# Induced-set attention with a maxout layer: maxima swapped by GpSimd, a column of ones beside x, and a short softmax kept in PSUM

## The chip, the cores and the metric

The kernel runs on one core of a Trainium2 chip. The metric is the device time of one execution in microseconds, as a median over runs. Below, PE is TensorE's matrix unit, PEld its loading of weights, DVE is VectorE, ACT is ScalarE, POOL is GpSimd and SP is SyncE, which here only issues DMAs.

## The reference

Four batches of 12544 tokens with 128 channels attend to 32 inducing points, which have first attended to the tokens; a maxout layer of width 768 follows. All of it is float32.

```python
B, N, m, C = (4, 12544, 32, 128)

def mab(q, kv):
    s = scale * (q @ kv.transpose(0, 2, 1))
    s = s - s.max(-1, keepdims=True)
    a = np.exp(s)
    a /= a.sum(-1, keepdims=True) + 1e-09
    return a @ kv
h = mab(I, x)        # I: the inducing points, for every batch
y = mab(x, h)        # tokens attend to the 32 states
# maxout, d_model 128, d_ff 768, on the 50176 rows of y
g = np.maximum(np.maximum(y @ w1, y @ w2), y @ w3)
out = g @ w_out
```

## The kernel before

**Tiles.** A batch has 98 tiles of 128 tokens: a short group of 2 tiles and 6 full groups of 16. x comes twice from HBM: as tokens (`xg`, tokens on partitions) and, for batches 1 to 3, already transposed by the host (`xT`, channels on partitions). For batch 0 PE transposes it. The host changes no value.

**First attention, batch 0 (`phase1_first`).** Before the pipeline starts, groups are taken one by one: load, transpose on PE (`transpose_x`, L270), scores, maxima, exponentials, sums. In between, DVE prepares the weights in a fixed order. Loads are queued in the order `LOADS`. Then the second attention's softmax for the short group and the first full one runs in an order written out by hand (`ORDER`); steps "a" are the short group's, "b" the full one's.

**Main pipeline (`main`, `advance`, `stage2`).** The two halves of the layer are folded, so that a chunk of 512 tokens needs no y: `us` holds the states multiplied by w1 - w2 and w3 - w2, and by the product of w2 and w_out. The 600 slots are 6 blocks of 128 of the layer for each of 100 chunks. In each slot PE multiplies `pu` of the next slot (L758) and `pv` of this one (L764); ACT makes `ru` = relu(pu) (L773); DVE makes `h` = max(pv, ru) (L791); ACT rounds h to `hi` (L780); POOL makes the remainder `lo` = h - hi (L788), or DVE does so in the slots of `LOWVEC` (L794). Six slots later PE adds three products of hi and lo into the chunk's sum (L814 to L816), which L813 has started in the chunk's first slot. `pu`, `pv` and the chunk's sum `acc` have two PSUM banks each; `h` has five buffers, hi and lo have ten.

**Windows.** A window is 24 slots: the four chunks of one full group. In each the next group's softmax goes through DVE and ACT one step at a time (`softmax2` at the slots of `STEPS2`, steps in `scores_steps`), and its result is spread over partitions by SP's DMAs (`probs`, L743). The short group has its own form of the last steps, and a copy of its scores in SBUF (`es`).

**Turns.** The first attention of batches 1 to 3 runs inside the windows, one group (the first turn two groups) at a time, 6 turns a batch, 18 in all. `turn` puts its steps at fixed slots from the window's slot 2 on (for batch 1 also from slot 15): scores on PE (`turn_products`, L363), a negated copy with its minimum per partition (`turn_max`, L381), then the minimum over the four blocks of 32 partitions by two exchanges (`turn_swap` with 64 and then 32 partitions, L401 and L402; `turn_least`, L409 and L413), exponentials (`turn_weights`, L422), a transpose of 32 x 32 blocks (`turn_transpose`, L434). A window later the weighted sums follow (`turn_sums`, L448), and the running sums are rescaled (`turn_keep`: `hs` L463 for the states, `ls` L466 for the sums of weights). At a batch's end `turn_totals` (L479, L480) adds up the blocks. The last batch's windows have no turns.

The order on every engine is the program's own (a manual schedule): an instruction that waits holds all that is behind it on its engine.

Of the kernel before, what the change touches and what calls it, by code (L numbers as in the profile page):

```python
# [8 lines left out]
F32 = mybir.dt.float32  # L9
# [4 lines left out]
ALU = mybir.AluOpType  # L14
# [11 lines left out]
def kernel(ctx, tc, x, xt, ind_t, w1, w2, w3, w_out, out):  # L26
# [43 lines left out]
    xp = ctx.enter_context(tc.tile_pool(name="xp", bufs=2))  # L70
# [36 lines left out]

    xg_next = {}
    xts_free = [const.tile([P, GT * P], F32, name=f"xT{i}", tag=f"xT{i}") for i in range(XTB)]
    xgs_free = [const.tile([P, GT, C], F32, name=f"xg{i}", tag=f"xg{i}") for i in range(XB)]  # L110
    w_space = xts_free.pop()
    shelf = const.tile([P, UW + 2 * groups[0]["nt"] * P + 2 * P + 2 * M + OB * 512], F32, name="shelf")
    shelf_at = [0]

    def place(n):
# [123 lines left out]

    def start_batch(b):  # L240
        st = state[b] = {"xT": {}, "xg": {}, "a": {}, "s": {}}
        st["lst"] = bp.tile([P, NG], F32, name="lst", tag="lst")
        if b == 0:
            st["mneg"] = bp.tile([P, NG], F32, name="mneg", tag="mneg", bufs=1)
            st["hg"] = bp.tile([P, NG, C], F32, name="hg", tag="hg", bufs=1)
        else:
            st["mm"] = bp.tile([P, NK], F32, name="mm", tag="mm")
            st["fac"] = bp.tile([P, NK], F32, name="fac", tag="fac")
            st["hs"] = bp.tile([P, C], F32, name="hs", tag="hs")
            st["ls"] = bp.tile([P, 1], F32, name="ls", tag="ls")  # L250
# [14 lines left out]
    def transpose_x(b, gi, k):  # L265
        st = state[b]
        n = min(4, groups[gi]["nt"] - k)
        tps = (bank_u + bank_v)[k // 4]
        for i in range(n):
            nc.tensor.transpose(out=tps[:, i * P : (i + 1) * P], in_=st["xg"][gi][:, k + i, :], identity=ident)  # L270
# [60 lines left out]
    def attend_sums(b, gi, bank=None):  # L331
        nt = groups[gi]["nt"]
        st = state[b]
        xg, aT = st["xg"].pop(gi), st["a"].pop(gi)
        if nt == GT:
            xgs_free.append(xg)
        st["h"] = hps = bank or spare[0]
        for t in range(nt):
            q = t % NQ
            nc.tensor.matmul(  # L340
                out=hps[q * M : (q + 1) * M, :C],
                lhsT=aT[:, t * M : (t + 1) * M],
                rhs=xg[:, t, :],
                start=(t < NQ),
                stop=(t + NQ >= nt),
            )
# [8 lines left out]
    def turn_products(b, k):  # L355

        st = state[b]
        banks = {}
        for gi in turns[k]:
            w = groups[gi]["nt"] * M  # L360
            bank = bank_a[1] if groups[gi]["nt"] == GT else spare[0][:, C : C + w]
            for q in range(NQ):
                nc.tensor.matmul(  # L363
                    out=bank[q * M : (q + 1) * M, :w],
                    lhsT=iT,
                    rhs=st["xT"][gi][:, q * w : (q + 1) * w],
                    start=True,
                    stop=True,
                )
            banks[gi] = bank[:, :w]  # L370
        st[("s", k)] = banks

    def turn_max(b, k):

        st = state[b]
        a = wk.tile([P, WK], F32, name="a", tag="a")
        mq = wk.tile([P, 3], F32, name="mq", tag="mq")
        at = 0
        for i, (gi, bank) in enumerate(st.pop(("s", k)).items()):
            w = bank.shape[1]  # L380
            nc.vector.tensor_scalar(  # L381
                out=a[:, at : at + w],
                in0=bank,
                scalar1=-1.0,
                scalar2=None,
                op0=ALU.mult,
                op1=ALU.min,
                accum_out=mq[:, i : i + 1],
            )
# [4 lines left out]
        st[("mq", k)] = mq[:, :1], mq[:, 2:]  # L394

    def turn_swap(b, k, step):

        st = state[b]
        mq, other = st[("mq", k)]
        for lo in range(0, P, 2 * step):  # L400
            nc.vector.tensor_copy(out=other[lo : lo + step], in_=mq[lo + step : lo + 2 * step])  # L401
            nc.vector.tensor_copy(out=other[lo + step : lo + 2 * step], in_=mq[lo : lo + step])  # L402

    def turn_least(b, k, last):

        st = state[b]
        mq, other = st[("mq", k)]
        if not last:
            nc.vector.tensor_tensor(out=mq, in0=mq, in1=other, op=ALU.min)  # L409
        elif k == 0:  # L410
            nc.vector.tensor_tensor(out=st["mm"][:, :1], in0=mq, in1=other, op=ALU.min)
        else:
            nc.vector.scalar_tensor_tensor(  # L413
                out=st["mm"][:, k : k + 1], in0=mq, scalar=st["mm"][:, k - 1 : k], in1=other, op0=ALU.min, op1=ALU.min
            )

    def turn_weights(b, k):

        st = state[b]
        a = st[("a", k)]  # L420
        least = st["mm"][:, k : k + 1]
        nc.scalar.activation(out=a, in_=a, func=AF.Exp, bias=least, scale=-1.0, accum_out=st["lst"][:, k : k + 1])  # L422
# [14 lines left out]
    def turn_sums(b, k):  # L437
# [7 lines left out]
        st["h"] = spare[0][:, :C]  # L445
        for t, row in enumerate(rows):
            q = t % NQ
            nc.tensor.matmul(  # L448
# [7 lines left out]
    def turn_keep(b, k):  # L456

        st = state[b]
        if k == 0:
            nc.vector.tensor_copy(out=st["hs"], in_=st["h"])  # L460
            return
        fac = st["fac"][:, k : k + 1]
        nc.vector.scalar_tensor_tensor(  # L463
            out=st["hs"], in0=st["hs"], scalar=fac, in1=st["h"], op0=ALU.mult, op1=ALU.add
        )
        nc.vector.scalar_tensor_tensor(  # L466
            out=st["ls"],
            in0=st["ls"] if k > 1 else st["lst"][:, :1],
            scalar=fac,
            in1=st["lst"][:, k : k + 1],  # L470
            op0=ALU.mult,
            op1=ALU.add,
        )
# [206 lines left out]
    def scores_steps(b, gi):  # L680
# [181 lines left out]
    def turn(b, k, s):  # L862

        at(s, turn_products, b, k)
        at(s + 2, turn_max, b, k)
        at(s + 3, turn_swap, b, k, 2 * M)
        at(s + 4, turn_least, b, k, False)
        at(s + 5, turn_swap, b, k, M)
        at(s + 6, turn_least, b, k, True)
        at(s + 7, turn_weights, b, k)  # L870
        at(s + 9, turn_transpose, b, k)

    def window(i):
        return (i // (NG - 1)) * per_batch + short + (i % (NG - 1)) * WIN
# [18 lines left out]
    for n in range(1, B):  # L893
# [144 lines left out]
```

## Time and profile before

| | |
|---|---|
| median of 3 runs | 851.65 us (850.05 to 854.28) |
| profiled execution | 854.22 us, of which span 852.4 us |
| PE, ACT, DVE, POOL busy | 96%, 87%, 79%, 75% |
| granted TensorE clock | 0.991 |
| loads of x (L94) | 23 of 1024 KB, 4 of 256 KB, 4 of 128 KB |

The span runs from the first to the last instruction of one profiled execution. A group line names line, engine, operation, tiles and shapes, then the busy time, the mean of one in ns, and the idle time of the engine just before them with what ended it. A timeline row starts with start and duration in us. Matmuls are pipelined and their ends are modelled, so PE's start times say more than its busy time.

### The profile page before, as it was taken

The page shows a single profiled execution, that of the slowest core. Times are in us where ns is not written, and L with a number is a line of the kernel's source. Part 1 is how long each engine was busy: PE and PEld are TensorE (multiplying, and loading weights), DVE is VectorE, ACT ScalarE, POOL GpSimd, SP SyncE. Part 2 cuts the span into 40 slices and gives each one's busy share as a digit, 9 for nine tenths or more (in the row PEclk, how much of TensorE's full clock was granted, in tenths as well). Part 3 has the DMA queues.
Part 4 walks back from the last instruction along what each step waited for, and adds up shares of the span by engine and source line. Part 5 has one row for each costly group of instructions (what it writes and reads, how often), then busy time and mean ns, then how long its engine had stood idle before and what let it go on. Part 6 is the DMA issues. An engine that isn't in the chain of part 4 may idle for free.

```text
span 852.4 us, 14763 instructions
## 1 busy us (share of the span) xinstructions
PE 821.6 (96%) x4530; PEld 623.8 (73%) x4530; DVE 675.7 (79%) x1238; ACT 744.3 (87%) x1508; POOL 636.2 (75%) x509
## 2 busy tenths in 40 slices
PE   6879999999999999999999999999999999999998
PEld 4646776777777777777677677777778778778786
DVE  5958788787886977878888779788788788777864
ACT  5748898988988989989889789898899899999996
POOL 0027687877877878878768778787789888888886
PEclk9979999999999999999999999999999999999999
DMA  9406643335453343353355343431423222222221
GB/s 345 163 22 201 211 164 109 122 105 170 123 151 120 102 159 121 102 179 119 97 155 161 119 130 100 167 121 48 131 71 93 75 75 67 64 75 75 72 77 50
DMA packets 44061, 102.50 MB, mean 120 GB/s; under 512 B 9552, under 2 KB 13264, under 8 KB 38736
## 3 DMA queue, kind: packets, MB, share of 16 engines
q1 hardware_dynamic: 43984, 101.57, 37.1%
q8 instruction: 36, 0.59, 0.3%
q14 instruction: 41, 0.34, 0.1%
HBM read 48.12 MB, written 25.69 MB: 87 GB/s over the span
## 4 chain that ended last, share of the span: by engine, by line
PE 78%; DVE 15%; issue 3%; ACT 2%; POOL 1%; DMA 1%; SPq 0%; DVEq 0%; ACTq 0%; POOLq 0%
PE pv L764 14%; PE acc L814 14%; PE acc L815 13%; PE acc L816 13%; PE pu L758 13%; DVE h L791 5%; PE aux L675 3%; PE acc L813 2%; PE acc L448 2%; PE aux L363 2%; DVE aux L695 1%; DVE a L381 1%; DVE mx L693 1%; DVE mq L401 1%; DVE mq L402 1%
## 5 line engine op out<-in xcount | busy, mean ns | idle before, releaser
L788 POOL TENSOR_TENSOR lo<-h,hi 128x512 fp32r<-128x512 f32 (+1 forms) x498 | 630.9, 1296 | 157.4 <-ACT hi L780 100.0
L791 DVE TENSOR_TENSOR h<-pv,ru 128x512 f32<-128x512 f32 (+1 forms) x600 | 401.8, 673 | 142.9 <-PE pv L764 93.4
L773 ACT ACTIVATE ru<-pu 128x512 f32<-128x512 f32 (+1 forms) x600 | 372.2, 620 | 59.5 <-PE pu L758 56.0
L780 ACT CAST hi<-h 128x512 fp32r<-128x512 f32 (+1 forms) x600 | 383.2, 639 | 15.6 <-DVE h L791 12.9
L764 PE MATMUL pv<-pT,us 128*128 128x512 f32 (+1 forms) x600 | 238.4, 397 | 12.2 <-DVE h L791 11.4
L758 PE MATMUL pu<-pT,us 128*128 128x512 f32 (+1 forms) x600 | 232.8, 388 | 3.3 <-ACT hi L780 1.9
L814 PE MATMUL acc<-hi,wo_hi 128*128 128x512 f32 (+1 forms) x600 | 235.4, 392 | 0.0
L815 PE MATMUL acc<-hi,wo_lo 128*128 128x512 f32 (+1 forms) x600 | 232.0, 387 | 0.0
L816 PE MATMUL acc<-lo,wo_hi 128*128 128x512 f32 (+1 forms) x600 | 231.7, 386 | 0.0
L764 PEld LDWEIGHTS pv<-pT,us 128*128 128x128 f32 x600 | 112.8, 188 | 54.8 <-DVE h L791 34.5
L814 PEld LDWEIGHTS acc<-hi,wo_hi 128*128 128x128 f32 x600 | 113.0, 188 | 40.6 <-issue 20.5
L758 PEld LDWEIGHTS pu<-pT,us 128*128 128x128 f32 x600 | 112.8, 188 | 30.1 <-ACT ru L773 2.3
L816 PEld LDWEIGHTS acc<-lo,wo_hi 128*128 128x128 f32 x600 | 112.9, 188 | 23.5
L815 PEld LDWEIGHTS acc<-hi,wo_lo 128*128 128x128 f32 x600 | 113.0, 188 | 22.4
L794 DVE TENSOR_TENSOR lo<-h,hi 128x512 fp32r<-128x512 f32 x102 | 73.9, 725 | 1.8 <-ACT hi L780 1.0
L821 ACT COPY shelf<-acc 128x512 f32<-128x512 f32 (+1 forms) x100 | 61.0, 610 | 3.0 <-PE acc L816 3.0
L813 PE MATMUL acc<-pT,us 128*128 128x512 f32 (+1 forms) x100 | 39.0, 390 | 0.0
L234 POOL TENSOR_TENSOR wo_lo<-xT,wo_hi 128x768 fp32r<-128x768 f32 x1 | 1.8, 1806 | 39.0 <-ACT wo_hi L233 39.0
L675 PE MATMUL aux<-xT,hT 128*32 128x512 f32 x192 | 26.4, 623 | 0.0
L448 PEld LDWEIGHTS acc<-xg,aT 128*32 128x32 f32 x576 | 16.8, 110 | 8.5 <-issue 5.5
L813 PEld LDWEIGHTS acc<-pT,us 128*128 128x128 f32 x100 | 18.9, 190 | 3.2
L723 DVE TENSOR_TENSOR pl<-aux,ph 128x512 fp32r<-128x512 f32 x24 | 16.5, 688 | 4.2 <-ACT ph L720 4.2
(136 smaller groups left out, 476.3 us busy)
## 6 DMA issues: line engine op xcount, KB each, us to landing
out_dram<-shelf SPq DMA_DIRECT2D x96, 256.0 KB, 2.0
xg<-in_x_dram SPq DMA_DIRECT2D x23, 1024.0 KB, 5.3
xT<-in_xt_dram SPq DMA_DIRECT2D x18, 1024.0 KB, 5.1
pT<-ph SPq DMA_DIRECT2D x192, 64.0 KB, 2.0
pT<-pl SPq DMA_DIRECT2D x192, 64.0 KB, 2.0
raw<-in_w_dram SPq DMA_DIRECT2D x3, 768.0 KB, 11.7
us<-uh SPq DMA_DIRECT2D x24, 52.0 KB, 2.5
us<-ul SPq DMA_DIRECT2D x24, 52.0 KB, 1.9
```

The costliest lines, as they stand in the source:

```text
L758: nc.tensor.matmul(out=pu[:, :w], lhsT=state[c.b]["us"][:, 2 * j * P : (2 * j + 1) * P], rhs=c.pT[:, :w], start=True, stop=True)
L764: nc.tensor.matmul(out=pv[:, : d.w], lhsT=state[d.b]["us"][:, (2 * j + 1) * P : (2 * j + 2) * P], rhs=d.pT[:, : d.w], start=True, stop=True,)
L773: nc.scalar.activation(out=ru[:, :w], in_=pu[:, :w], func=AF.Relu)
L780: nc.scalar.copy(out=hi[:, : c.w], in_=h[:, : c.w])
L788: nc.gpsimd.tensor_sub(**args)
L791: nc.vector.tensor_max(out=h[:, : d.w], in0=pv[:, : d.w], in1=relus.pop(s)[:, : d.w])
L794: nc.vector.tensor_sub(**low)
L813: nc.tensor.matmul(out=c.acc[:, :w], lhsT=us[:, 2 * DF :], rhs=c.pT[:, :w], start=True, stop=False)
L814: nc.tensor.matmul(out=c.acc[:, :w], lhsT=wo_hi[:, j, :], rhs=c.hh[j][:, :w], start=False, stop=False)
L815: nc.tensor.matmul(out=c.acc[:, :w], lhsT=wo_lo[:, j, :], rhs=c.hh[j][:, :w], start=False, stop=False)
L816: nc.tensor.matmul(out=c.acc[:, :w], lhsT=wo_hi[:, j, :], rhs=c.hl[j][:, :w], start=False, stop=(j == NJ - 1))
L821: nc.scalar.copy(out=o[:, : c.w], in_=c.acc[:, : c.w])
```

## The change

Three things are changed together.

1. **Swaps on GpSimd.** The six copies of a turn's exchange go from DVE to POOL. `mq` has room beside each column for what comes from the other block, so that each minimum is one `tensor_reduce` over adjacent columns; in the last one a third column, copied by POOL too, holds the minimum of the turn before. The separate minimum of a turn with two groups is gone. The steps after the first swap move back: the two minima from slots +4 and +6 to +5 and +8, the second swap from +5 to +6, the weights from +7 to +9, the transpose from +9 to +11.
2. **A column of ones.** The tiles of tokens become 129 columns wide, the last set to 1 once at the start, so the loads fill rows of 512 B that are 516 B apart. The turn's weighted sums take all 129 columns, so the last column of `hs` is the sum of weights; `ls`, its rescaling and the accumulating output of the exponentials are gone. The short group's tokens move from a pool of their own to the shelf.
3. **Short softmax in PSUM.** The scores of the short group are transposed in place and stay in PSUM, and its last steps (for batches 1 to 3) come up to three slots earlier.

```diff
+    for xg in xgs_free + [short_x]:
+        nc.gpsimd.memset(xg[:, :, C:], 1.0)
...
-            nc.sync.dma_start(out=xg[:, k : k + n, :], in_=xv[b, :, g["t0"] + k : g["t0"] + k + n, :])
+            nc.sync.dma_start(out=xg[:, k : k + n, :C], in_=xv[b, :, g["t0"] + k : g["t0"] + k + n, :])
...
-        mq = wk.tile([P, 3], F32, name="mq", tag="mq")
+        n = 2 * len(turns[k])
+        mq = wk.tile([P, n + 3], F32, name="mq", tag="mq")
...
-        if len(turns[k]) > 1:
-            nc.vector.tensor_tensor(out=mq[:, :1], in0=mq[:, :1], in1=mq[:, 1:2], op=ALU.min)
+        if k > 0:
+            nc.gpsimd.tensor_copy(out=mq[:, n + 2 :], in_=st["mm"][:, k - 1 : k])
...
     def turn_swap(b, k, step):
-        mq, other = st[("mq", k)]
-        for lo in range(0, P, 2 * step):
-            nc.vector.tensor_copy(out=other[lo : lo + step], in_=mq[lo + step : lo + 2 * step])
-            nc.vector.tensor_copy(out=other[lo + step : lo + 2 * step], in_=mq[lo : lo + step])
+        n = len(turns[k])
+        own, far = (mq[:, :n], mq[:, n : 2 * n]) if step > M else (mq[:, 2 * n : 2 * n + 1], mq[:, 2 * n + 1 : 2 * n + 2])
+        for lo in range(0, P, step):
+            to = lo ^ step
+            nc.gpsimd.tensor_copy(out=far[to : to + step], in_=own[lo : lo + step])
...
     def turn_least(b, k, last):
-        if not last:
-            nc.vector.tensor_tensor(out=mq, in0=mq, in1=other, op=ALU.min)
...
-            nc.vector.scalar_tensor_tensor(
-                out=st["mm"][:, k : k + 1], in0=mq, scalar=st["mm"][:, k - 1 : k], in1=other, op0=ALU.min, op1=ALU.min
-            )
+        n = 2 * len(turns[k])
+        out, cols = (st["mm"][:, k : k + 1], mq[:, n : n + 2 + (k > 0)]) if last else (mq[:, n : n + 1], mq[:, :n])
+        nc.vector.tensor_reduce(out=out, in_=cols, axis=AX.X, op=ALU.min)
...
-        nc.scalar.activation(out=a, in_=a, func=AF.Exp, bias=least, scale=-1.0, accum_out=st["lst"][:, k : k + 1])
+        nc.scalar.activation(out=a, in_=a, func=AF.Exp, bias=least, scale=-1.0)
...
-        nc.vector.scalar_tensor_tensor(
-            out=st["ls"],
-            in0=st["ls"] if k > 1 else st["lst"][:, :1],
...
-        nc.tensor.matmul(out=st["lp"], lhsT=st["ls"].to_broadcast([P, P]), rhs=sel[:, :M], start=True, stop=True)
+        nc.tensor.matmul(out=st["lp"], lhsT=st["hs"][:, C:].to_broadcast([P, P]), rhs=sel[:, :M], start=True, stop=True)
...
-        if nt < GT:
-            flat = wk.tile([P, w], F32, name="es", tag="es", bufs=1)
...
-        nc.vector.transpose(out=flat, in_=sp[:, :w])
+        nc.vector.transpose(out=flat, in_=flat)
...
-        at(s + 4, turn_least, b, k, False)
-        at(s + 5, turn_swap, b, k, M)
-        at(s + 6, turn_least, b, k, True)
-        at(s + 7, turn_weights, b, k)
-        at(s + 9, turn_transpose, b, k)
+        at(s + 5, turn_least, b, k, False)
+        at(s + 6, turn_swap, b, k, M)
+        at(s + 8, turn_least, b, k, True)
+        at(s + 9, turn_weights, b, k)
+        at(s + 11, turn_transpose, b, k)
...
-        softmax2(n, 0, *(s0 + k for k in (17, 18, 19, 20, 21, 22, 23, 24, 26, 28)))
+        softmax2(n, 0, *(s0 + k for k in (17, 18, 19, 20, 21, 22, 23, 23, 24, 25)))
```

More of the change, by code (lines that the diff above doesn't have):

```diff
@@ L109 @@
     xts_free = [const.tile([P, GT * P], F32, name=f"xT{i}", tag=f"xT{i}") for i in range(XTB)]
-    xgs_free = [const.tile([P, GT, C], F32, name=f"xg{i}", tag=f"xg{i}") for i in range(XB)]
+    xgs_free = [const.tile([P, GT, C + 1], F32, name=f"xg{i}", tag=f"xg{i}") for i in range(XB)]
     w_space = xts_free.pop()
-    shelf = const.tile([P, UW + 2 * groups[0]["nt"] * P + 2 * P + 2 * M + OB * 512], F32, name="shelf")
+    shelf = const.tile([P, UW + 2 * groups[0]["nt"] * P + 2 * P + 2 * M + OB * 512 + groups[0]["nt"] * (C + 1)], F32, name="shelf")
     shelf_at = [0]
@@ L120 @@
     short_t = [place(groups[0]["nt"] * P) for i in range(2)]
+    short_x = place(groups[0]["nt"] * (C + 1)).rearrange("p (t c) -> p t c", c=C + 1)
+    for xg in xgs_free + [short_x]:
+        nc.gpsimd.memset(xg[:, :, C:], 1.0)
     iT = place(M)
@@ L241, in start_batch @@
         st = state[b] = {"xT": {}, "xg": {}, "a": {}, "s": {}}
-        st["lst"] = bp.tile([P, NG], F32, name="lst", tag="lst")
         if b == 0:
+            st["lst"] = bp.tile([P, NG], F32, name="lst", tag="lst", bufs=1)
             st["mneg"] = bp.tile([P, NG], F32, name="mneg", tag="mneg", bufs=1)
@@ L269, in transpose_x @@
         for i in range(n):
-            nc.tensor.transpose(out=tps[:, i * P : (i + 1) * P], in_=st["xg"][gi][:, k + i, :], identity=ident)
+            nc.tensor.transpose(out=tps[:, i * P : (i + 1) * P], in_=st["xg"][gi][:, k + i, :C], identity=ident)
         xv4 = st["xT"][gi].rearrange("p (q t l) -> p t q l", q=NQ, l=M)
@@ L342, in attend_sums @@
                 lhsT=aT[:, t * M : (t + 1) * M],
-                rhs=xg[:, t, :],
+                rhs=xg[:, t, :C],
                 start=(t < NQ),
@@ L360, in turn_products @@
             w = groups[gi]["nt"] * M
-            bank = bank_a[1] if groups[gi]["nt"] == GT else spare[0][:, C : C + w]
+            bank = bank_a[1] if groups[gi]["nt"] == GT else spare[0][:, 2 * C : 2 * C + w]
             for q in range(NQ):
@@ L390, in turn_max @@
             at += w
-        if len(turns[k]) > 1:
-            nc.vector.tensor_tensor(out=mq[:, :1], in0=mq[:, :1], in1=mq[:, 1:2], op=ALU.min)
         st[("a", k)] = a[:, :at]
-        st[("mq", k)] = mq[:, :1], mq[:, 2:]
+        if k > 0:
+            nc.gpsimd.tensor_copy(out=mq[:, n + 2 :], in_=st["mm"][:, k - 1 : k])
+        st[("mq", k)] = mq
     def turn_swap(b, k, step):
-        st = state[b]
-        mq, other = st[("mq", k)]
-        for lo in range(0, P, 2 * step):
-            nc.vector.tensor_copy(out=other[lo : lo + step], in_=mq[lo + step : lo + 2 * step])
-            nc.vector.tensor_copy(out=other[lo + step : lo + 2 * step], in_=mq[lo : lo + step])
+        n = len(turns[k])
+        mq = state[b][("mq", k)]
+        own, far = (mq[:, :n], mq[:, n : 2 * n]) if step > M else (mq[:, 2 * n : 2 * n + 1], mq[:, 2 * n + 1 : 2 * n + 2])
+        for lo in range(0, P, step):
+            to = lo ^ step
+            nc.gpsimd.tensor_copy(out=far[to : to + step], in_=own[lo : lo + step])
     def turn_least(b, k, last):
         st = state[b]
-        mq, other = st[("mq", k)]
-        if not last:
[L409 to L413, printed above, removed]
-                out=st["mm"][:, k : k + 1], in0=mq, scalar=st["mm"][:, k - 1 : k], in1=other, op0=ALU.min, op1=ALU.min
-            )
+        n = 2 * len(turns[k])
+        mq = st[("mq", k)]
+        out, cols = (st["mm"][:, k : k + 1], mq[:, n : n + 2 + (k > 0)]) if last else (mq[:, n : n + 1], mq[:, :n])
+        nc.vector.tensor_reduce(out=out, in_=cols, axis=AX.X, op=ALU.min)
     def turn_weights(b, k):
@@ L444, in turn_sums @@
                 xgs_free.append(xg)
-        st["h"] = spare[0][:, :C]
+        st["h"] = spare[0][:, : C + 1]
         for t, row in enumerate(rows):
@@ L465, in turn_keep @@
         )
-        nc.vector.scalar_tensor_tensor(
-            out=st["ls"],
-            in0=st["ls"] if k > 1 else st["lst"][:, :1],
[L469 to L473, printed above, removed]
     def turn_totals(b, bank):
@@ L478, in turn_totals @@
         st["lp"], st["sum"] = bank[:, :M], bank[:, M : 2 * M]
-        nc.tensor.matmul(out=st["lp"], lhsT=st["ls"].to_broadcast([P, P]), rhs=sel[:, :M], start=True, stop=True)
-        nc.tensor.matmul(out=st["sum"], lhsT=st["hs"], rhs=sel[:, :M], start=True, stop=True)
+        nc.tensor.matmul(out=st["lp"], lhsT=st["hs"][:, C:].to_broadcast([P, P]), rhs=sel[:, :M], start=True, stop=True)
+        nc.tensor.matmul(out=st["sum"], lhsT=st["hs"][:, :C], rhs=sel[:, :M], start=True, stop=True)
     def phase1_first(weights):
```

6 lines of the change are left out of this document (2 added, 4 removed).

## The prediction

> **What bounds the kernel now.** I read the page first: engine shares, the chain, the groups.
>
> ```profile
> span 852.4 us, 14763 instructions
> PE 821.6 (96%) x4530; PEld 623.8 (73%) x4530; DVE 675.7 (79%) x1238; ACT 744.3 (87%) x1508; POOL 636.2 (75%) x509
> PE 78%; DVE 15%; issue 3%; ACT 2%; POOL 1%; DMA 1%; SPq 0%; DVEq 0%; ACTq 0%; POOLq 0%
> ```
>
> PE is the bound, but 15% of the chain is DVE, so PE waits for it somewhere. A busy PE is no proof of a dense one, so next I compared stretches: a full window (24 slots, one group of tokens) of batch 1, with a turn in it, and one of batch 3, which has none. The timeline's pv records mark where each starts and ends, and the two PE bursts are what a turn adds.
>
> ```profile
> 302.38 0.39 PE L764 MATMUL pv<-pT,us 128*128 128x512 f32 x1
> 335.02 0.39 PE L764 MATMUL pv<-pT,us 128*128 128x512 f32 x1
> 728.16 0.39 PE L764 MATMUL pv<-pT,us 128*128 128x512 f32 x1
> 757.52 0.39 PE L764 MATMUL pv<-pT,us 128*128 128x512 f32 x1
> 306.08 1.06 PE L448 MATMUL acc<-xg,aT 128*32 128x128 f32 x32
> 306.95 1.04 PE L363 MATMUL aux<-xT,shelf 128*32 128x512 f32 x8
> 302.40:335.00 32.60, 32.02 (x173) 24.03 (x172) 26.25 (x50) 29.07 (x59) 25.54 (x21) 1.00 0.40 129
> 728.20:757.50 29.30, 29.30 (x133) 23.32 (x132) 23.17 (x38) 27.93 (x56) 24.60 (x20) 1.00 0.25 73
> ```
>
> The window with a turn takes 335.02 - 302.38 = 32.64 us, the one without 757.52 - 728.16 = 29.36. PE's own work for the turn is 1.06 + 1.04 = 2.10, so 32.64 - 29.36 - 2.10 = 1.18 us is standing. The waits of that window (engine, line, releaser, total, times, longest) and DVE's timeline show where.
>
> ```profile
> PEld pv L764 <- DVE h L791: 1.9, 4, 0.9
> 310.36 5.25 POOL L788 TENSOR_TENSOR lo<-h,hi 128x512 fp32r<-128x512 f32 x4 [2.46 <-PE pu L758]
> 310.97 0.70 DVE L466 SCALAR_TENSOR_TENSOR ls<-ls,fac,lst 128x1 f32<-128x1 f32 x1
> 314.25 0.15 DVE L402 COPY mq<-mq 64x1 f32<-64x1 f32 x1
> 314.43 0.69 DVE L791 TENSOR_TENSOR h<-pv,ru 128x512 f32<-128x512 f32 x1
> 315.04 0.58 DVE L409 TENSOR_TENSOR mq<-mq 128x1 f32<-128x1 f32 x1
> 315.55 0.68 DVE L791 TENSOR_TENSOR h<-pv,ru 128x512 f32<-128x512 f32 x1
> ```
>
> PE waits for h, because pv's two banks come free only when h has read them. L409 works on one column, yet takes 0.58 us and ends at 315.62; POOL's fourth lo ends at 310.36 + 5.25 = 315.61. It stood for POOL. Its range over the run says the same, beside the copies (one input) and the reduction (one input, no wait):
>
> ```profile
> L409 DVE TENSOR_TENSOR mq<-mq x18: 234/580/1300, 74.5 to 582.9; 128x1 f32<-128x1 f32 x18
> L402 DVE COPY mq<-mq x54: 143/147/149, 73.7 to 585.2; 32x1 f32<-32x1 f32 x36, 64x1 f32<-64x1 f32 x18
> L308 DVE TENSOR_REDUCE mneg<-acc x7: 154/156/163, 6.9 to 39.9; 128x1 f32<-128x4 f32 x7
> ```
>
> **The change part by part.** *DVE loses.* Six copies a turn, 6 x 0.147 = 0.88 us; L409 (0.58) and the last minimum L413, both for reductions of 0.16; and L466 (0.70), as the ones column carries the sums of weights through hs.
>
> ```profile
> L413 DVE SCALAR_TENSOR_TENSOR mm<-mq,mm 128x1 f32<-128x1 f32 x15 | 5.7, 383 | 0.0
> L422 ACT ACTIVATION_READ_ACCUMULATOR a<-a,mm 128x1 f32 x18 | 3.4, 186 | 0.0
> L448 PE MATMUL acc<-xg,aT 128*32 128x128 f32 x576 | 19.6, 273 | 0.0
> ```
>
> That is 0.88 + 0.58 + 0.38 + 0.70 - 2 x 0.16 = 2.2 us of DVE a turn, 40 us over 18 turns. It counts only where it ends PE's wait: 18 x 1.18 = 21.2 us at most. ACT sheds 0.186 us a turn (3.4 in all), off the path. The merged minimum of the two-group turns goes with it. Row 129 of L448 costs 19.6/128 = 0.15 us in all; hs with 129 columns nothing.
>
> *POOL gains* six copies of one or two columns a turn and, from k = 1, one more of the old minimum. No row shows such a copy. Bounds: a memset of one column (0.10, nothing read), and what is left at zero width of POOL's two-input lo, from its two forms.
>
> ```profile
> 0.27 0.10 POOL L1018 MEMSET const-float32-1.0<- 128x1 f32 x1
> L788 POOL TENSOR_TENSOR lo<-h,hi 128x512 fp32r<-128x512 f32 x474 | 612.4, 1321 | 153.2 <-ACT hi L780 96.5 <-PE pu L758 43.0 <-PE pv L764 9.4
> L788 POOL TENSOR_TENSOR lo<-h,hi 128x256 fp32r<-128x256 f32 x24 | 18.6, 794 | 4.2 <-ACT hi L780 3.5 <-PE pu L758 0.6
> ```
>
> 0.794 - (1.321 - 0.794) = 0.27. A copy reads one input and carries little, so I take 0.15, nearer the memset. Seven add 1.05 us to a window in which POOL is busy 25.5 of 32.6, but behind them queue the lo products. These follow each other every 5.25/4 = 1.31 us at most, against 1.13 us of a slot on PE (below), so POOL falls behind through slots 3 to 14 anyway. A lo has room: it is made one slot after its h and used six slots after, so the copies should cost PE nothing there.
>
> *The new wait* is DVE's: each reduction stands for POOL's swap, and behind it stand h products. The first swap (issued in slot 5, read in slot 7) arrives in time. The second is issued in slot 8 behind lo of slot 7 and read in slot 10. The POOL row above begins with lo of slot 2, so lo of slot 5 ends at 315.61:
>
> ```profile
> 311.27 0.39 PE L764 MATMUL pv<-pT,us 128*128 128x512 f32 x1
> 300.12 0.39 PE L764 MATMUL pv<-pT,us 128*128 128x512 f32 x1
> 301.25 0.39 PE L764 MATMUL pv<-pT,us 128*128 128x512 f32 x1
> 300.64 0.69 DVE L791 TENSOR_TENSOR h<-pv,ru 128x512 f32<-128x512 f32 x1 [0.38 <-PE pv L764]
> ```
>
> That is 4.34 after its pv (311.27). An undisturbed slot takes 301.25 - 300.12 = 1.13, and 1.36 where a chunk's sum begins (once in slots 5 to 7), so lo of slot 7 ends 4.34 + 2 x 0.18 - 0.23 + 3 x 0.15 = 4.9 after its pv, and the swap 0.6 later, 5.5. Slot 10's pv comes at 3.4 on that count, and its h ends 0.52 + 0.69 later, at 4.6. DVE stands 0.9 us, and h of slot 11, due at 3.4 + 1.13 + 0.52 = 5.05, starts at 5.7, 0.65 late. PE forgives h about 1.0 us: two slots (2.26) less 0.52 and 0.69.
>
> But the reciprocal and the product of the softmax follow in slot 11 and now both transposes in slot 13 (the weights' one moved from slot 11), and ACT, busy 29.07 of 32.60, has little left. So I leave 0.35 us of stall a turn: 18 x 0.35 = 6.3. At 0.10 a copy h is 0.3 late and nothing is left (0); at 0.27 it is 1.5 late, over PE's allowance before the softmax's work comes on top, and about all of 1.18 stays (21).
>
> *Short softmax in PSUM.* It matters at the start, on the chain:
>
> ```profile
> 53.68 1.19 DVE L713 TENSOR_TENSOR pn<-es,pn 128x128 fp32r<-128x128 f32 x1 [1.05 <-ACT pn L711]
> L463 DVE SCALAR_TENSOR_TENSOR hs<-hs,fac,acc x15: 303/306/340, 122.7 to 610.3; 128x128 f32<-128x128 f32 x15
> ```
>
> With one input from PSUM I price it like L463, 0.31: -0.9 us (0 if it keeps its 1.19). In later batches it ends a window before it is wanted.
>
> *x loads.* A row of tokens becomes 516 B apart, so a load of 8 KB a partition becomes 16 pieces of 512 B. No row shows 512 B. These stretches hold loads in 8 KB pieces, in 1 KB pieces (w_out), and the run of the first loads (us, engines' busy and counts, clock, DMA share, GB/s):
>
> ```profile
> 14.00:16.20 2.20, 2.20 (x16) 1.96 (x14) 2.17 (x4) 1.45 (x4) 0.00 (x0) 1.00 0.98 408
> 11.70:13.70 2.00, 2.00 (x10) 0.35 (x3) 0.13 (x1) 0.84 (x3) 0.00 (x0) 1.00 1.14 403
> 2.00:9.00 7.00, 3.55 (x21) 2.85 (x22) 2.76 (x8) 1.50 (x5) 0.00 (x0) 1.00 0.95 330
> 9.00:25.00 16.00, 14.39 (x121) 9.53 (x119) 11.85 (x20) 12.05 (x27) 0.00 (x0) 1.00 0.97 389
> 25.00:33.50 8.50, 8.50 (x120) 5.99 (x116) 8.36 (x14) 6.95 (x16) 0.00 (x0) 1.00 0.69 264
> 26.33 0.87 PE L270 MATMUL pu<-shelf,xg 128*128 128x128 f32 x6
> ```
>
> At full share 408/0.98 = 416 GB/s over 16 engines is 315 ns per 8 KB, and 403/1.14 = 353 is 46 ns per 1 KB. A line through both gives 8 ns a piece and 0.0375 ns a byte, so 27 ns for 512 B: 16 x 27 = 435 ns for 315, +1.0 us per 1 MB group. The ends: 20 ns (no price per piece) and 46 (a piece of 512 B no cheaper than one of 1 KB).
>
> Before, 7 x 330 + 16 x 389 = 8.5 MB are in by 25 us: the weights (3.1) and x through group 5 (5.4). Five groups then land 4.7 us later. Group 5's transposes start at 26.33, so 1.3 us of that is slack. From 25 to 33.5 DVE is busy 8.36 of 8.5 with weight preparation in fixed order and absorbs about another 1.1. I take +2.3 us (0 to +15, at 46 ns). Steady loads of x run slots ahead, at a DMA share of 0.40: nothing. The six memsets of ones precede the identity on POOL, about 0.6 us before its first use at 4 us: nothing, +0.5 if loads wait for them.
>
> The Trainium skill (DMA: Bandwidth & Descriptors, Specifications) gives 512 B as the least transfer at line rate; by it the x loads would cost 0 and the sum 2.3 less. No run here shows a 512 B piece yet.
>
> **Sum**, on the profiled execution (854.22 us; span 852.4): -21.2 + 6.3 + 0.15 - 0.9 + 2.3 = -13.4, so 840.8. The median of the three runs is 2.6 lower, 851.65: 838.2, say 838.
>
> **The rivals.** (1) *All stalls go*: copies at 0.10, POOL never late. For it, POOL stands idle 153 us before lo. Against it, the arithmetic of slot 10. 838.2 - 6.3 - 2.3/2 = 831.
>
> (2) *The wait moves to POOL*: copies at 0.27, DVE stands for swaps as long as it stood for the port. 18 x 1.18 comes back: 851.65 - 0.9 + 2.3 + 0.15 = 853. So the change would then not do what it says. POOL's 1.3 us lo in front of every swap speaks for it; the cheap memsets against.
>
> (3) *Pieces at odd addresses*: 516 is no multiple of anything wide. If each piece touches a quarter more, 34 ns, a group costs +1.8 us, group 5 lands 9 us late, group 6 about 8, of which DVE's order absorbs 2: +6.0 in place of +2.3, 842. No row shows a load to addresses like these, so none excludes it. The Trainium skill (DMA: Bandwidth & Descriptors, How a descriptor splits into AXI transactions) says that a descriptor off a 256 B boundary fetches from the boundary below; that is where such a quarter could come from.
>
> (4) *Slower*: the same place, a piece at twice its 27 ns (each end written in two goes), 54 ns. A group then takes +4.4 us, group 6 lands 23 us late and the first part ends 21 later: 838.2 - 2.3 + 21 = 857. It decides from 46 ns on, where the delay is +15 and the gain is gone. Against it: 46 ns buys twice the bytes.
>
> **How the numbers follow.** Forecast 0.52; (1) 0.13; (2) 0.12; (3) 0.15; (4) 0.08. Half a per cent (4.3 us) is what a measurement tells from no change: 847.4 to 855.9. Faster: 0.52 + 0.13 + 0.13 of (3) = 0.78. Same: most of (2), and the rest of (3): 0.11. Slower: (4) and 0.03 of (2): 0.11. The range 829 to 851 holds the forecast, (1), (3) and a milder (2). The forecast's own is 832 to 845.
>
> **What would show it.** Windows of batch 1 at 31.5 to 31.9 us in place of 32.64, those of batch 3 unchanged. PE's waits for h at under a third. POOL copies at 100 to 200 ns, 123 of them; the reductions at 0.16 with waits for POOL of about 0.9 in front of the second alone. The first pv at 57 to 58 us where it was 56.26:
>
> ```profile
> 56.26 0.28 PE L764 MATMUL pv<-pT,us 128*128 128x256 f32 x1
> ```
>
> Packets up by some 46,000. The prediction fails if copies on POOL take over 0.25 us, if pieces take over 34 ns, or if ACT, not DVE, holds PE once DVE is free.

## The result, and the profile after

The changed kernel takes 838.63 us (median of 4 runs, 838.14 to 840.12), the kernel before beside it 850.85 us (849.45 to 854.28). The ratio is 0.9853, 95% interval 0.982 to 0.9887, 12 us less; 838 was forecast. The profiled execution takes 838.18 us. All times are medians of the fast runs; the one run left out is of e5, at 1626.8 us, and no trace tells why it took so long.

Below are the page's first lines of the changed kernel, and its chain. DVE's part of the chain has gone from 15% to 3%, PE's from 78% to 89%.

```profile
span 836.2 us, 14865 instructions
...
PE 813.5 (97%) x4530; PEld 623.7 (75%) x4530; DVE 652.6 (78%) x1112; ACT 738.6 (88%) x1490; POOL 667.0 (80%) x638
...
PE 89%; POOL 3%; DVE 3%; SPq 2%; ACT 1%; DMA 1%; issue 1%; DVEq 0%; POOLq 0%; ACTq 0%
```

The waits over the whole run (us in total, times, longest), first PE's for h before, then after, and the new wait of the second minimum for POOL:

```profile
PEld pv L764 <- DVE h L791: 34.5, 66, 1.1
```

```profile
PEld pv L752 <- DVE h L779: 13.3, 43, 0.9
DVE mm L413 <- POOL mq L405: 20.3, 18, 1.8
```

The groups of the moved work. POOL's copies take 183 and 186 ns, DVE's minima 143 and 156, and nearly all of DVE's waiting stands before the second minimum: 20.3/18 = 1.13 us a turn.

```profile
L405 POOL COPY mq<-mq 32x1 f32<-32x1 f32 (+2 forms) x108 | 19.8, 183 | 5.2
L395 POOL COPY mq<-mm 128x1 f32<-128x1 f32 x15 | 2.8, 186 | 0.0
L413 DVE TENSOR_REDUCE mm<-mq 128x1 f32<-128x3 f32 (+1 forms) x18 | 2.8, 156 | 20.3 <-POOL mq L405 20.3
L413 DVE TENSOR_REDUCE mq<-mq 128x1 f32<-128x2 f32 (+1 forms) x18 | 2.6, 143 | 0.3 <-POOL mq L405 0.3
```

The windows again, one row each. In these rows stand a window's pv multiplications, 25 of them with the next window's first, their shortest, median and longest in ns, and the start of the first and of the last, so that the last two numbers are the window's ends (where the text gives a window to 0.01 us, it is from the timeline's single starts). Batch 1 before, then after; batch 3 before, then two of after.

```profile
L764 PE MATMUL pv<-pT,us x25: 387/389/504, 302.4 to 335.0; 128*128 128x512 f32 x25
L764 PE MATMUL pv<-pT,us x25: 388/389/393, 728.2 to 757.5; 128*128 128x512 f32 x25
```

```profile
L752 PE MATMUL pv<-pT,us x25: 388/389/486, 323.6 to 355.2; 128*128 128x512 f32 x25
L752 PE MATMUL pv<-pT,us x25: 389/395/398, 709.9 to 739.7; 128*128 128x512 f32 x25
L752 PE MATMUL pv<-pT,us x25: 389/398/398, 769.7 to 799.6; 128*128 128x512 f32 x25
```

Batch 1's window falls from 32.64 to 31.54 us, by 1.10. But batch 3's, in which no turn runs and none of the changed code, grows from 29.36 to 29.79 and 29.97: PE itself is slower there, 395 to 398 ns for an operation of 389. The prediction had these windows unchanged, and half of the experiments below are about them.

### The profile page after: what moved, and what is told of

Its sections match the earlier page's. It is cut to its first block, busy times and chain, and to the rows that moved or that the text cites. A ratio compares the mean times of both kernels' runs of the same rounds, so it can differ in the third digit from the quotient of the medians.

```text
span 836.2 us, 14865 instructions
## 1 busy us (share of the span) xinstructions
PE 813.5 (97%) x4530; PEld 623.7 (75%) x4530; DVE 652.6 (78%) x1112; ACT 738.6 (88%) x1490; POOL 667.0 (80%) x638
## 2 busy tenths in 40 slices
DMA packets 46111, 102.51 MB, mean 123 GB/s; under 512 B 9552, under 2 KB 15824, under 8 KB 40784
## 4 chain that ended last, share of the span: by engine, by line
PE 89%; POOL 3%; DVE 3%; SPq 2%; ACT 1%; DMA 1%; issue 1%; DVEq 0%; POOLq 0%; ACTq 0%
PE acc L802 16%; PE pv L752 16%; PE pu L746 15%; PE acc L803 15%; PE acc L804 15%; PE aux L665 3%; PE acc L801 3%; POOL lo L776 2%; PE acc L446 2%; PE aux L364 2%; SPq L128 2%; DMA xg<-in_x_dram 1%; DVE h L779 1%; SPq L93 1%; ACT ru L761 0%
## 5 line engine op out<-in xcount | busy, mean ns | idle before, releaser
L776 POOL TENSOR_TENSOR lo<-h,hi 128x512 fp32r<-128x512 f32 (+1 forms) x498 | 640.5, 1318 | 106.5 <-PE pu L746 48.4
L761 ACT ACTIVATE ru<-pu 128x512 f32<-128x512 f32 (+1 forms) x600 | 367.6, 613 | 63.4 <-PE pu L746 57.3
L768 ACT CAST hi<-h 128x512 fp32r<-128x512 f32 (+1 forms) x600 | 376.7, 628 | 1.5 <-DVE h L779 1.0
L752 PEld LDWEIGHTS pv<-pT,us 128*128 128x128 f32 x600 | 113.0, 188 | 34.7 <-DVE h L779 13.3
L782 DVE TENSOR_TENSOR lo<-h,hi 128x512 fp32r<-128x512 f32 x102 | 99.0, 970 | 1.9 <-ACT hi L768 1.0
L405 POOL COPY mq<-mq 32x1 f32<-32x1 f32 (+2 forms) x108 | 19.8, 183 | 5.2
```

Of the source, the lines that this page charges most:

```text
L752: nc.tensor.matmul(out=pv[:, : d.w], lhsT=state[d.b]["us"][:, (2 * j + 1) * P : (2 * j + 2) * P], rhs=d.pT[:, : d.w], start=True, stop=True,)
L761: nc.scalar.activation(out=ru[:, :w], in_=pu[:, :w], func=AF.Relu)
L768: nc.scalar.copy(out=hi[:, : c.w], in_=h[:, : c.w])
L776: nc.gpsimd.tensor_sub(**args)
L782: nc.vector.tensor_sub(**low)
```

## The experiments

My theory after the comparison: the gain is the one predicted (DVE's small two-input operations no longer stand for POOL), PE's loss in batch 3 comes from where the tiles lie in SBUF, and the start loses some 3 us to x in 512 B pieces. The rivals: it is the number of DVE's operations that counted; PE's loss comes from the 129th column; POOL has room to spare.

**One part at a time.** Three kernels, each the kernel before with one of the three parts.

```diff
 # e1: turn_max, turn_swap, turn_least of the change, and its later slots
-        at(s + 4, turn_least, b, k, False)
...
+        at(s + 5, turn_least, b, k, False)
+        at(s + 6, turn_swap, b, k, M)
+        at(s + 8, turn_least, b, k, True)
+        at(s + 9, turn_weights, b, k)
+        at(s + 11, turn_transpose, b, k)
 # e2: 129 columns and hs instead of ls; swaps and slots as before
+    xgs_free = [const.tile([P, GT, C + 1], F32, name=f"xg{i}", tag=f"xg{i}") for i in range(XB)]
 # e3: the short group's scores stay in PSUM
+        nc.vector.transpose(out=flat, in_=flat)
```

> The kernel before with the first part alone: swaps on POOL, each minimum one reduction, the later slots. The loads of x, ls (L466) and the short softmax are as before. Theory (DVE's small two-input operations stand for POOL and make h late; the swaps and minima carry most of it): the middle windows of batch 1, 32.64 us before and 31.54 with the whole change, come to 31.6 to 31.9, the first pv stays near 56, and the time is some 16 us under the kernel before, 835, so under the whole change, which pays 3.4 us for slower loads of x. Rival (the sums of weights, L466, were the wait that counted, as they come first in the window): windows stay at 32.2 or more and the time at 844.

> The second part alone: rows of x 516 B apart, the column of ones, no ls and no accumulator read; swaps and minima on DVE in the old slots, the short softmax as before. Theory: DVE is 0.6 us earlier from slot 3 on, but L409 still stands for POOL, so the middle windows of batch 1 fall from 32.64 to about 32.1 and 18 turns give 9 us; the loads of x cost 3.4 us at the start: 845. Rival (L466 was the wait that counted): windows 31.6 and 836 to 838. Rival for the loads: hidden behind the weight preparation, then 3 us less in each case.

> The third part alone: the short softmax in PSUM. Theory: the last subtraction takes 0.3 us where it took 1.2 to 1.4, 0.9 us less on the chain before the first pv, nothing later, as the later batches' short groups are done long before they are wanted: 0.9 us under the kernel before, about 850, no change that can be told. Rival: the windows with a short softmax (34.5 us before) were held by it too: 0.5 us less in each, 848.

The kernel before is at 851.0 us here. Swaps alone: 836.75, ratio 0.9829 (0.9807 to 0.9851). The column of ones alone: 854.56, ratio 1.0043 (1.0027 to 1.0059), slower, where I had expected 845. The short softmax alone: 849.7, ratio 0.9985 (0.9969 to 1.0002). -14.25 + 3.56 - 1.3 = -12.0: the parts add up to the whole, and the second one costs. Rows of e1, a window of batch 1 and the group of ls, and then of e2, a window of batch 1, one of batch 3, and the group of the first minimum, with the same group of the kernel before:

```profile
L761 PE MATMUL pv<-pT,us x25: 388/389/449, 291.3 to 323.3; 128*128 128x512 f32 x25
```

```profile
L463 DVE SCALAR_TENSOR_TENSOR ls<-ls,fac,lst 128x1 f32<-128x1 f32 x12 | 8.8, 734 | 0.0
```

```profile
L757 PE MATMUL pv<-pT,us x25: 387/389/504, 300.9 to 333.3; 128*128 128x512 f32 x25
L757 PE MATMUL pv<-pT,us x25: 389/395/398, 726.5 to 756.3; 128*128 128x512 f32 x25
```

```profile
L410 DVE TENSOR_TENSOR mq<-mq 128x1 f32<-128x1 f32 x18 | 15.4, 853 | 0.0
```

```profile
L409 DVE TENSOR_TENSOR mq<-mq 128x1 f32<-128x1 f32 x18 | 11.2, 623 | 0.0
```

With the swaps moved and ls left, a window takes 32.0 us and ls still takes 0.73 for one column; without it 31.54 (the whole change). With ls gone and the old minima left, the first of these takes 853 ns where it took 623: the wait for POOL's lo moves to the next operation with two inputs in SBUF. So e2's window falls only by 0.3 us, from 32.64 to 32.36, though a ls of 0.70 is gone, and it shows the slower PE of batch 3 (29.8 us, 395 ns) without any swap on POOL. The Trainium skill (SBUF — State Buffer, Who interferes with whom) says that a VectorE instruction with two SBUF inputs contends with a GpSimd instruction that reads SBUF, and one with a single SBUF input, outside the two-port modes, does not. The trace agrees: 853 and 734 ns for one column with two inputs, 143 to 156 for a reduction of two or three.

**Whole rows for batch 0's x.** The whole change, but batch 0's tiles of x are laid out as 128 columns and the column of ones is set when a later batch takes the place.

```diff
+        if b == 0:
+            xg = flat[:, : g["nt"] * C].rearrange("p (t c) -> p t c", c=C)
+        else:
+            xg = flat.rearrange("p (t c) -> p t c", c=C + 1)
+            if id(flat) not in ones:
+                ones[id(flat)] = flat
+                nc.gpsimd.memset(xg[:, :, C:], 1.0)
```

> The whole change, but batch 0's tokens lie in rows of 512 B without gaps in the same tiles (batch 0 has no use for the ones); the ones are set on POOL before each tile's first load of batch 1. Theory (the x loads in 512 B pieces are on the path at the start): group 5 lands at 25 us again, the minimum over all groups (43.5 us in the whole change, 40.1 before) comes 3.4 us earlier, the first pv at 52, and the time is 3.4 us under the whole change, 835. Rival (the loads hide behind the weight preparation on DVE): first pv at 55.4, the time within 0.5 us of the whole change.

835.28 us, ratio 0.9807 (0.9783 to 0.9831), 3.35 less than the whole change, as the theory had it. The intervals of the two ratios overlap, so the rows below carry this more than the medians do. The first pv comes at 53.2 us, 2.2 earlier and not 3.4; in this execution the clock stood at 0.50 from 46.4 to 49.8 us, before it. The stretch of the first loads (us, the engines' busy time, clock, share of the DMA engines, GB/s) and the start of the minimum that closes the first attention, changed kernel and then e4:

```profile
9.00:25.00 16.00, 12.27 (x74) 7.46 (x72) 10.81 (x17) 9.96 (x23) 0.00 (x0) 1.00 1.01 319
25.00:33.50 8.50, 6.48 (x86) 5.02 (x90) 6.81 (x11) 5.53 (x13) 0.00 (x0) 1.00 0.94 285
```

```profile
L543 DVE TENSOR_REDUCE mmin<-mneg x1: 159/159/159, 43.5 to 43.5; 128x1 f32<-128x7 f32 x1
```

```profile
9.00:25.00 16.00, 14.37 (x122) 9.72 (x120) 12.23 (x20) 12.12 (x27) 0.00 (x0) 1.00 0.97 388
```

```profile
L551 DVE TENSOR_REDUCE mmin<-mneg x1: 160/160/160, 40.1 to 40.1; 128x1 f32<-128x7 f32 x1
```

With all DMA engines at work in both, 388/0.97 = 400 GB/s become 319/1.01 = 316, and the minimum comes 3.4 us later.

**Thirty-two bytes.** In the built programs the column of ones moves all tiles behind the shelf; they then start at 32 bytes past a multiple of 64, where before they started at one. Three kernels move them by 32 bytes: the changed one (e8), the one before (e9), and e4 (e10). The edit of e8:

```diff
-    ... + groups[0]["nt"] * (C + 1)], F32, name="shelf")
+    ... + groups[0]["nt"] * (C + 1) + 8], F32, name="shelf")
```

> The changed kernel with eight more floats (32 bytes of each partition) in its shelf, nothing else: the first x buffer and every tile placed behind it stand 32 bytes further on, at multiples of 64 bytes as in the kernel before. Theory (PE's wider matmul pitch from slot 370 on, 230 to 233 ns in place of 227, comes from where the column of ones put the tiles): batch 3's windows go from 29.8 to 29.97 back to 29.37 us, and the time from 838.6 to about 835.3. Rival (the pitch comes from the 129th column itself, or from what the chip draws in power): windows of batch 3 stay at 29.8 to 29.97, time 838.6.

> The kernel before with the same eight floats in its shelf, so that its tiles stand where they stood, but 32 bytes off a multiple of 64. Theory (addresses): windows of batch 3 go from 29.37 to 29.8 or 29.97 us, time from 851 to about 854. Rival: no change, 29.37 and 851.

> The changed kernel with batch 0's x read in whole rows and the column of ones set behind it (as in the earlier kernel at 835.28 us), and the eight floats besides. Theory: both leftovers add, 835.3 less 3.3 gives about 832, windows of batch 3 at 29.37 us. Rival: the addresses do nothing, 835.3.

839.27, 851.2 and 835.67 us beside 850.12: nothing moves. Ratios 0.9867 (0.984 to 0.9894), 1.0003 (0.9988 to 1.0019), 0.9821 (0.9793 to 0.9848). A window of batch 3 in e8, and in e9:

```profile
L752 PE MATMUL pv<-pT,us x25: 389/395/398, 711.0 to 740.8; 128*128 128x512 f32 x25
```

```profile
L764 PE MATMUL pv<-pT,us x25: 388/389/389, 728.0 to 757.4; 128*128 128x512 f32 x25
```

This form of the theory falls: a shift of all tiles together is nothing to PE. What these kernels leave alone is how the tiles stand to each other.

**Swaps and short softmax without the column of ones.**

> The kernel before with the swaps and minima of the change and its short softmax, without the column of ones. Theory (the parts add): 836.75 less 0.9 to 1.3 for the short softmax gives 835.5 to 835.9, with batch 1's windows at 32.0 us and batch 3's at 29.37. Rival: the short softmax's microsecond is absorbed before the first pv, 836.8.

835.89 us, ratio 0.9829 (0.98 to 0.9858), batch 1's windows at 32.0 and batch 3's at 29.4. The two parts without the column of ones are worth as much as all three.

**Where the tiles stand to each other.** From slot 371 of 600 on, at 543 us, PE's pitch (from the start of one multiplication to the next) in the changed kernel goes from 227 ns to between 230 and 233, so a slot of five takes 1.15 to 1.17 us in place of 1.13; the pv of two stretches, one on each side:

```profile
L752 PE MATMUL pv<-pT,us x34: 387/389/472, 495.7 to 537.9; 128*128 128x512 f32 x34
L752 PE MATMUL pv<-pT,us x29: 388/394/413, 545.2 to 581.5; 128*128 128x512 f32 x29
```

By the built program the probabilities pT of chunk 62 (slot 372), and later batch 3's us, then move into the places of x buffers that are finished, and five x buffers have grown by 64 bytes each. So pT then stands 320 bytes off from where it stood, against the tiles of the upper region. The changed kernel holds a control of its own: by the built program pT of chunk 64 alone, between chunks 62 and 87, stays in the upper region at the old distance. The pv of chunks 63, 64 and 65:

```profile
L752 PE MATMUL pv<-pT,us x6: 393/396/398, 551.0 to 560.0; 128*128 128x512 f32 x6
L752 PE MATMUL pv<-pT,us x6: 388/389/393, 561.1 to 567.0; 128*128 128x512 f32 x6
L752 PE MATMUL pv<-pT,us x6: 394/396/413, 568.2 to 574.3; 128*128 128x512 f32 x6
```

Two kernels turn this about: e12 keeps the x and xT buffers' places taken to the end, so that nothing moves into them; e13, which has no column of ones, puts 320 unused bytes between the regions.

```diff
 # e12, on the changed kernel; the last two lines stand behind its last work
+    xgs_all = list(xgs_free) + [t.rearrange("p (t c) -> p t c", c=P) for t in xts_free]
...
+        for xg in xgs_all:
+            nc.gpsimd.memset(xg[:, :1, P - 1 : P], 1.0)
 # e13, on the kernel with swaps and short softmax (e11)
-            st["hg"] = bp.tile([P, NG, C], ...)
+            st["hg"] = bp.tile([P, NG * C + 80], ...)[:, : NG * C].rearrange("p (g c) -> p g c", c=C)
```

> The changed kernel with five one-column writes to the x buffers and seven to the xT buffers by POOL behind its last work, so that these buffers' places stay taken to the end: the chunks' probabilities (pT) of chunk 62 on, and batch 3's folded weights (us), no longer move into the places of finished x buffers. Nothing else is changed. Theory (PE's pitch of 230 to 233 ns from slot 371 on comes from where pT then stands against the tiles that the other engines use): the windows of batch 3 go from 29.8 and 29.97 us to 29.4, the time from 838.6 to about 835.5 and the writes' 1 us at the end. Rival (the place is nothing to it): windows 29.8 to 29.97, time 838.6 to 839.6.

> The kernel with the swaps and the short softmax, without the column of ones (835.89 us, windows of batch 3 at 29.37), with 320 bytes of each partition put between the x buffers and the tiles of the pipeline (the tile of batch 0's partial states is that much longer and nothing uses the rest). The column of ones makes the five x buffers 320 bytes longer together, so that the two regions then stand to each other as in the changed kernel. Theory (the distance of the two regions sets the pitch): windows of batch 3 at 29.8 to 29.97 us, time about 839. Rival (the distance is nothing to it): 29.37 and 835.9.

e12: 834.2 us, ratio 0.9799 (0.9777 to 0.9822), the lowest median of all kernels here; the changed kernel's interval (0.982 to 0.9887) touches this one, so the rows below part the two better than the times. e13: 846.52, ratio 0.9936 (0.9915 to 0.9958), 10 us more than e11, where 839 was expected. Windows of batch 3 and of batch 1 in e12, then in e13:

```profile
L753 PE MATMUL pv<-pT,us x25: 388/389/389, 707.3 to 736.6; 128*128 128x512 f32 x25
L753 PE MATMUL pv<-pT,us x25: 388/389/489, 292.2 to 323.8; 128*128 128x512 f32 x25
```

```profile
L759 PE MATMUL pv<-pT,us x25: 388/392/398, 715.7 to 745.6; 128*128 128x512 f32 x25
L759 PE MATMUL pv<-pT,us x25: 388/394/492, 292.9 to 325.0; 128*128 128x512 f32 x25
```

Both go as the theory said, e13 further. Its median pv of batch 1 takes 394 ns already, so PE is slower from the start and not from slot 371 on. There hi and lo, too, stand 320 bytes off from their weights. The cause of the wider pitch is thus shown to be the places of tiles, in both directions: e13 adds no work at all, e12 only writes behind the last work, and e12 keeps the 129th column, so that rival falls. Of e13's 10 us the profiled executions show 5.3 (842.0 and 836.7 us of span, e13's fastest run and e11's slowest); where the rest goes no trace tells. The size in the changed kernel can be read from the pv rows of the whole run, first to last start: before, changed, e12.

```profile
L764 PE MATMUL pv<-pT,us x600: 277/389/628, 56.3 to 842.9; 128*128 128x512 f32 x144, 128*128 128x256 f32 x6
```

```profile
L752 PE MATMUL pv<-pT,us x600: 276/392/628, 55.4 to 827.0; 128*128 128x512 f32 x144, 128*128 128x256 f32 x6
```

```profile
L753 PE MATMUL pv<-pT,us x600: 277/389/628, 55.7 to 822.0; 128*128 128x512 f32 x144, 128*128 128x256 f32 x6
```

That is 786.6, 771.6 and 766.3 us: the turns gave 20.3, and the places took 5.3 of it back. (The shifted kernels e9 and e8, the same pipelines as the first two, have 786.7 and 771.7.)

**Copies on DVE after all.** The changed kernel with all seven copies of a turn on DVE.

```diff
-            nc.gpsimd.tensor_copy(out=mq[:, n + 2 :], in_=st["mm"][:, k - 1 : k])
+            nc.vector.tensor_copy(out=mq[:, n + 2 :], in_=st["mm"][:, k - 1 : k])
...
-            nc.gpsimd.tensor_copy(out=far[to : to + step], in_=own[lo : lo + step])
+            nc.vector.tensor_copy(out=far[to : to + step], in_=own[lo : lo + step])
```

> The changed kernel with the swaps' copies and the copy of the last minimum on DVE in place of POOL; its slots and its one-input minima stay. Tells apart whether taking the copies from DVE or taking two-input operations from it made the gain. Theory (the two-input minima that stand for POOL's lo were the price; a copy is 0.147 us): DVE gets 7 x 0.147 = 1.0 us a turn and loses the wait for POOL of 1.1, so batch 1's windows stay at 31.3 to 31.7 us and the time at 836 to 842. Rival (the number of DVE's operations in a turn is the price): windows of 32.2 us and more, time 850 or more.

843.53 us, ratio 0.9905 (0.9885 to 0.9925): 5 more than the change, just outside what I expected. Of e6, an ordinary window of batch 1, the window with the first turn, which takes two groups, the copies by duration, and the engines' busy time in the ordinary window (PE, PEld, DVE, ACT, POOL, with the number of operations); then, from the changed kernel, the window with the first turn; then, from e6's timeline, the two copies of 64 partitions by 2 columns in that window, and POOL's lo beside them.

```profile
L752 PE MATMUL pv<-pT,us x25: 388/389/397, 295.6 to 327.1; 128*128 128x512 f32 x25
L752 PE MATMUL pv<-pT,us x25: 387/389/501, 390.0 to 424.2; 128*128 128x512 f32 x25
L405 DVE COPY mq<-mq x108: 141/147/1240, 71.8 to 569.7; 32x1 f32<-32x1 f32 x72, 64x1 f32<-64x1 f32 x30, 64x2 f32<-64x2 f32 x6
295.60:327.10 31.50, 31.50 (x174) 24.39 (x173) 25.05 (x50) 28.59 (x58) 25.61 (x22) 1.00 0.45 135
```

```profile
L752 PE MATMUL pv<-pT,us x25: 387/389/397, 386.7 to 419.5; 128*128 128x512 f32 x25
```

```profile
398.03 5.05 POOL L776 TENSOR_TENSOR lo<-h,hi 128x512 fp32r<-128x512 f32 x4 [2.56 <-PE pu L746]
401.31 1.80 DVE L405 COPY mq<-mq 64x2 f32<-64x2 f32 x2
```

The ordinary window is 31.44 us, as good as with POOL's copies: seven copies of 0.147 us cost DVE what its wait for POOL cost. DVE has 50 operations in it, as many as in the window of the kernel before (32.64 us), so their number was not the price. In an ordinary window, then, the place of the copies made no gain; the one-input minima, at their later slots, and the end of ls did. No run has the minima without the later slots. The loss is in the windows of the two-group turn (34.27 us against 32.85). There a copy has two columns; one takes up to 1.24 us, where one column takes 0.147, and the pair ends at 401.31 + 1.80 = 403.11, just as POOL's four lo end (398.03 + 5.05 = 403.08). By these ends it stood for POOL. The Trainium skill (VectorE: DVE Perf Modes, Mode 2×_2P — use both read ports for one tensor) says that a copy within SBUF can read through both ports when its outermost dimension longer than one is even; the copies of two columns are the only such ones here, and the only ones that stand.

**Twice the copies on POOL.**

```diff
+            for _ in range(2):
+                nc.gpsimd.tensor_copy(out=far[to : to + step], in_=own[lo : lo + step])
```

> The changed kernel with each of the six copies of a turn's swaps issued twice by POOL, to the same place. Tests how much more POOL's place in the chain could cost. Theory (DVE's wait before the second minimum grows by four more copies of 0.18 us to about 1.8, so that h of slot 11 is some 1.5 us late, and PE forgives about 1.0): batch 1's windows go from 31.53 to about 32.1 us, time 846 to 853. Rival (POOL has the room, since its copies stand between two remainders): windows 31.6 us, time 838 to 841.

863.83 us, ratio 1.015 (1.0123 to 1.0178), more than either theory gave. A window of batch 1, the second minimum's wait and PE's for h:

```profile
L753 PE MATMUL pv<-pT,us x25: 387/389/504, 305.1 to 338.0; 128*128 128x512 f32 x25
```

```profile
DVE mm L414 <- POOL mq L406: 46.3, 18, 3.2
PEld pv L753 <- DVE h L780: 40.5, 66, 1.9
```

The wait grows from 1.13 to 46.3/18 = 2.57 us, by 1.44, and the window from 31.54 to 32.97, by 1.43. I had let PE forgive part of that. It forgives nothing more: the change already uses all the room that this window has.

## Why the prediction was right

**Turns: right in mechanism, mis-sized, and covered by another error.** I put 21.2 us on the stalls' end and gave 6.3 back for what DVE's new wait leaves. The runs show 20.3 gained (e12), so 0.9 was left and not 6.3. Without other losses a turn's window is 29.33 (batch 3 in e12) + 2.10 = 31.4 us; it takes 31.54. The step that failed is the last one of the new wait: I had DVE stand 0.9 us and h of slot 11 0.65 late, inside PE's 1.0, and still added 0.35 for the softmax's steps and ACT. DVE stands 1.13 us, POOL's copy takes 0.183 and not 0.15, and PE's allowance holds even so. e5 shows how near its edge is. PE's waits for h fell from 34.5 to 13.3 us, to two fifths; under a third was the sign.

**A term that was missing: PE's own pitch, +5.3 us.** "Batch 3 unchanged" was among the signs, and it was wrong. 20.3 - 5.3 = 15.0 stands where the prediction had 21.2 - 6.3 = 14.9, so the forecast came true to 1 us by luck, by two errors of like size. Nothing in the profile of before could show it; what could have made me ask is that the change moves every tile.

**x loads: the price right, +3.4 us in place of +2.3.** The DMA records of the kept traces have 3,072 packets of 512 B in the changed kernel, from its loads of 256 and 128 KB, where the kernel before has none; they take 27 ns in the median. An 8 KB packet takes 438 to 455 ns in the median from 9 to 33 us, where it took 309 to 313. These are the 27 and 435 of the prediction, so neither a quarter more for odd addresses (rival 3) nor a doubling (rival 4) is there. (The 316 GB/s above would make it 8192 x 16 / 316 = 415 ns, but the stretch holds weights too, whose 6 KB packets stay at 234 to 240 ns.) No run has pieces of 512 B in rows without gaps, so a share of the addresses in the price is not excluded. Too large was what I let the chain absorb: DVE, which I had filling the delay with weight preparation, is busy 6.81 of 8.5 us where it was 8.36. The packet count was wrong as a sign: it goes from 44,061 to 46,111, and I had some 46,000 added. The 8 KB packets of the 1 MB loads stay in the count as they were; their pieces show in the time alone. By the Trainium skill's 512 B at line rate (DMA: Bandwidth & Descriptors, Specifications), which the prediction weighed, the loads would have cost nothing; 400 GB/s becoming 316 says otherwise here, for pieces that are also 516 B apart.

**Short softmax: as predicted.** L713 took 1.19 us at the start, and in the changed kernel its group is

```profile
L701 DVE TENSOR_TENSOR pn<-aux,pn 128x128 fp32r<-128x128 f32 x4 | 1.1, 283 | 0.4 <-ACT pn L699 0.4
```

0.9 was forecast, 1.3 us measured, with an interval that just reaches no change.

**The start as a sign: misread.** The first pv was to come at 57 to 58 us and comes at 55.4, though the loads cost more. The profiled execution of before had spent 10 us of its start at half clock, which the prediction did not look for (the clock is the third number from the right):

```profile
42.50:52.70 10.20, 9.61 (x60) 5.83 (x52) 4.36 (x15) 1.37 (x4) 0.00 (x0) 0.50 0.01 2
```

The medians carry less of this, so their difference is 12.2 us and the two profiled executions' 16.0.

**The rivals.** (1), all stalls gone, is nearest to what the turns did. (2), the wait moves to POOL, is half there: DVE stands 1.13 us a turn for POOL, but at a place where PE forgives nearly all of it. With twice the copies (e5) the whole stall is back and more. That DVE's number of operations was the price falls with e6. (3) and (4) fall with the 27 ns.

## What to carry to other kernels

A tiny operation that took far longer than its size says was waiting here, and the end of a neighbour's operation told for what: try it with one input and a single column before moving it to another engine. Taking such an operation away moved the wait to the next one (e2). When an edit changes the size of a buffer, compare the same instruction's time in stretches that the edit does not touch: where tiles stand to each other cost a quarter of what the turns gave. A part that looks free in a change should be timed alone; here the column of ones costs what it saves, through the places and the loads of x. No run has the column with both mended, as e4 and e12 together would.

## What the runs showed of the hardware

PE's rate depended on where its tiles lay. These groups are of about 89 us of batch 3, ACT and PE, before, then changed, then in e12, where the tiles keep their places:

```profile
L773 ACT ACTIVATE ru<-pu 128x512 f32<-128x512 f32 x72 | 45.8, 636 | 4.1 <-PE pu L758 3.7
L758 PE MATMUL pu<-pT,us 128*128 128x512 f32 x73 | 28.4, 389 | 0.0
```

```profile
L761 ACT ACTIVATE ru<-pu 128x512 f32<-128x512 f32 x72 | 43.7, 607 | 4.8 <-PE pu L746 3.8
L746 PE MATMUL pu<-pT,us 128*128 128x512 f32 x73 | 28.8, 394 | 0.0
```

```profile
L762 ACT ACTIVATE ru<-pu 128x512 f32<-128x512 f32 x72 | 45.8, 636 | 4.1 <-PE pu L747 3.7
L747 PE MATMUL pu<-pT,us 128*128 128x512 f32 x72 | 28.0, 389 | 0.0
```

While PE is slower, ACT is faster, 607 ns for 636, and both are back in e12; the granted clock is 1.00 in the stretches before and after. Whether they stand in each other's way no row tells. The Trainium skill (SBUF — State Buffer, Who interferes with whom) has PE and ACT wait for no other engine; the rows name no engine that PE waits for, so they do not settle this, and what they show is that some 5 ns in 227 of PE's pitch, and 29 ns of ACT's, go with the places of tiles. In the built programs, the tiles that PE reads stand multiples of 256 bytes apart wherever the pitch is narrow, and some stand 64 bytes off that (they were moved by 320) where it is wide. Which pair of tiles it is (PE's moving operand against the next weights, or either against ACT's), and whether other distances than 320 do the same, stays open; no run varied it.
